# Paired state products, 64x64 prefix sums of bf16 parts, a decay row through DRAM and a new hand-written order in a gated recurrence followed by a bilinear FFN

## The chip, the cores and the metric

One core of a Trainium2 chip runs the whole program. The metric is the device time of one execution in microseconds (us), smaller is better. The engines of the core are named as in the profile: PE (matrix multiply), PEld (its weight loads), DVE (vector), ACT (scalar/activation), POOL, and SP, which here only issues DMAs. PE writes into PSUM, which has 8 banks of 512 f32 columns on 128 partitions; the program numbers them 0 to 7.

## What is computed

A gated linear recurrence over time for 4 batches x 8 heads (768 steps, head size 48), and a bilinear feed-forward layer on its output:

```python
for t in range(S):
    state = alpha[:, :, t, :, None] * state + np.einsum('bhd,bhe->bhde', k[:, :, t], v[:, :, t])
    y[:, :, t] = np.einsum('bhd,bhde->bhe', q[:, :, t], state)
x = y.transpose(0, 2, 1, 3).reshape(B * S, H * D)      # 3072 x 384
return ((x @ w_a) * (x @ w_b)) @ w_out                 # d_ff 1536
```

## The kernel before

The 768 steps of each batch are worked on in six chunks, numbered 0 to 5. A chunk is one third of the time of two of the four batches (its two "rows" u = 0, 1): 256 steps, held as 128 partitions of 2 neighbouring steps (r = 0, 1). The 128 partitions are two halves g = 0, 1 of 64, and the state is carried from half to half and chunk to chunk. In each chunk:

- the logarithms of alpha are taken (`ln`, ACT), the two steps of a partition are added (`l2`, DVE), and prefix sums over the partitions of each half are taken on PE by a triangular matrix. Chunk 0 sums the logarithms themselves in f32 (`B`, `cum_both`); chunks 1 to 5 split the sums into a high part (`H`, `high`, rounded to f32r) and a low part (`L`, `low`), and multiply each by the 128x128 triangular matrix `utr` (`A2`, `cum2`, lines 625-628): two matmuls of 384 columns for each of the two rows;
- exponentials of the sums (`E`) scale k and q (`mk`, `mq` on DVE, after `lv` has set the two steps of a partition to one level, on DVE or POOL) into `QKp`. `QKp` is transposed either on PE (`C`, `Ce`) or, from chunk 2 on, by a DMA transpose on SP's queue (`T`);
- the decay of each half, a column of `bls`, comes from PE and ACT (`dk`, `de`) in chunks 0 and 1, and from chunk 2 on by two small writes to DRAM and two reads (`dr`, `dl`, all on SP's queue);
- products of k and v that update the state: `K` for one half at a time (`state_pe`), `K2` with the matmuls of the two halves alternating (`state_pe_both`); then `k` on DVE;
- scores `D`, masked either on DVE (`M`) or by a copy on ACT and a product on DVE (`Mc`, `Mm`); the output of the chunk in PSUM (`SB`, `SA`, `Y`), and its copy to `xT` (`X`);
- the feed-forward layer of the chunk: `a f` and `b f` (3 matmuls each for one of 12 column blocks of `w_a` or `w_b`; 512 columns for a whole chunk, written `*`, 256 for one row), a copy of a to SBUF (`as`, ACT), the product (`pr`, DVE), and `o m 0`, `o m 1` (6 matmuls of 384 columns each), copied out (`ot`) and stored (`st`).

PE forms: the feed-forward matmuls, `B`, `A2` and `C` use all of the 128x128 array; `K`, `K2`, `D`, `SB`, `SA`, `Y` use 64x64 tiles, of which several run side by side; `dk` uses 128x48.

Nothing is scheduled by a compiler: `PROGRAM` (lines 17-405) is a list of these operations in one hand-written order, "chunk: operation arguments". Each engine and each DMA queue takes its own operations from that list in that order, and waits for what an operation needs. The last letter says who does it (V = DVE, S = ACT, P = POOL, Y = SP); for PE operations the last number is the PSUM bank. So where an operation stands sets its place in its engine's queue, and a late input holds up everything behind it on that engine. SP's queue has all stores, the DMA transposes, the DRAM trips of the decays and some loads; POOL's queue has the other loads, the loads of the weights (`W`, `Wo`) and some `lv`.

Example, chunk 2's preparation before the change (lines 104-119, lines of other chunks left out):

```
2: L * V
...
2: A2 1 1
...
2: E 1 i
...
2: A2 0 7
...
2: E 0 i
```

The functions `cross` and `cum_quads` (lines 606-623) are in the kernel before, but its order has no call of them.

Of the kernel before, what the change touches and what calls it, by code (L numbers as in the profile page):

```python
# [233 lines left out]
2: b 10 * 5; as 9 *; a 10 * 6; b 7 * 3; pr 9 *; as 10 *; o 0 0 0; pr 7 *; pr 10 *
3: D 1 1 6; D 1 0 1
4: lv 1 k P
3: M 1 1
2: o 0 1 -
3: Mc 1 0
5: ld q * P  # L240
3: Mm 1 0 V; SB 0 3
2: ot 0 S
3: SB 1 1; D 0 1 5
4: lv 1 q V; A2 0 0
2: o 2 0 7
# [12 lines left out]
3: X 0 S; X 1 V
2: o 2 1 -
4: mq 0 V; A2 1 2  # L260
2: ot 2 S
3: a 2 * 5
5: l2 * V
3: b 4 * 3
4: E 1 b; E 0 i; E 1 i
3: b 3 * 4; a 4 * 7; b 2 * 2
4: v 1 S
3: as 2 *
4: dr
5: H * S  # L270
2: ot 3 S
5: ra 0
2: st 0 Y
4: mk 0 V
3: as 4 *
4: mk 1 V
2: st 2 Y
3: a 8 * 1
4: T 0
3: a 1 * 0; a 0 * 6; b 8 * 7; as 8 *; b 5 * 5; pr 2 *; pr 4 *  # L280
4: v 0 V; dl
5: lv 0 q V
3: pr 8 *
4: mq 1 V
5: lv 0 k V
3: as 0 *
5: ra 1
3: a 3 * 1; a 5 * 3; b 0 * 7; a 9 * 6; as 5 *; pr 5 *; a 7 * 3; a 11 * 5; pr 0 *; as 9 *; as 3 *; as 1 *
4: T 1
3: b 9 * 6; b 1 * 1  # L290
5: lv 1 q V
3: pr 9 *; a 6 * 2; pr 3 *; as 11 *; pr 1 *; as 6 *
4: K * 0 0; D 0 0 4
5: L * V
3: as 7 *; b 11 * 6; b 6 * 7; pr 11 *; a 10 * 1; pr 6 *
4: Mc 0 0
2: o 1 0 5
3: as 10 *
4: k * 0 V; D 1 0 3; D 1 1 6; D 0 1 1
5: v 1 S  # L300
4: Mc 1 0; M 1 1
5: A2 0 0
2: o 1 1 -
4: SB 0 6; Mc 0 1; Mm 0 0 V; SB 1 3
2: ot 1 V
5: A2 1 2
3: b 7 * 1
5: E 1 i; E 1 b; E 0 b
3: b 10 * 5
4: Mm 0 1 V; Mm 1 0 V  # L310
3: pr 7 *; o 1 0 2
5: mk 1 V
3: pr 10 *; o 2 0 1
5: mq 1 V
4: Y 1; SA 0
5: dr
2: st 3 Y
5: T 1
4: Y 0; SA 1; X 1 S
5: E 0 i  # L320
3: o 1 1 -; o 2 1 -
4: X 0 V
5: mk 0 V; mq 0 V
3: ot 1 S
4: a 6 * 0; a 7 * 5; as 6 *
5: T 0
4: b 6 * 3; as 7 *; a 1 * 6
5: dl
4: pr 6 *; a 0 * 5; b 7 * 7; pr 7 *
3: ot 2 V; st 1 Y  # L330
4: as 0 *; as 1 *; a 5 * 3; b 1 * 4; b 0 * 2
2: st 1 Y
3: st 2 Y
4: pr 1 *; as 5 *; pr 0 *
5: v 0 V
4: a 3 * 0; a 4 * 7; as 3 *
5: D 0 0 5
4: as 4 *
5: K * 0 4; M 0 0; D 1 1 2; D 1 0 0; Mc 1 1
3: o 3 0 7  # L340
5: k * 0 V; Mc 1 0
3: o 3 1 -
5: SB 1 5
3: ot 3 S
5: SB 0 3; D 0 1 0
4: b 10 * 2
3: o 0 0 7
5: M 0 1; Mm 1 0 V; Mm 1 1 V
4: b 3 * 1; b 4 * 0
3: o 0 1 -  # L350
4: pr 4 *; b 5 * 0
3: ot 0 S
5: SA 1
4: pr 5 *
5: Y 1; Y 0
4: pr 3 *
5: X 1 V; SA 0
4: a 2 * 7; a 10 * 6
5: X 0 S
4: as 10 *; as 2 *; a 8 * 5  # L360
5: a 4 * 3
4: b 2 * 0
3: st 0 Y
5: a 2 * 4
4: pr 2 *; as 8 *; a 9 * 7
5: b 2 * 1; a 11 * 0
4: pr 10 *; b 8 * 5
5: as 2 *; as 4 *; a 1 * 4
4: b 9 * 2; pr 8 *
5: pr 2 *; b 5 * 3; b 1 * 6  # L370
4: as 9 *
5: b 4 * 1; a 8 * 5
4: a 11 * 7
5: pr 4 *
4: pr 9 *
# [10 lines left out]
5: a 9 * 4  # L386
4: o 3 0 7
5: b 9 * 2; pr 3 *
4: ot 0 V; st 0 Y
3: st 3 Y  # L390
4: ot 1 S
5: as 9 *
# [645 lines left out]
```

## Time and profile before

| | us |
|---|---|
| median of 3 runs (lowest, highest) | 195.91 (194.92, 201.03) |
| the profiled execution's own time | 195.05 |
| its span, first to last instruction | 193.3 |
| PE busy | 187.9 |
| DVE busy | 132.9 |
| ACT busy | 106.3 |
| POOL busy | 51.4 |

The span is the time between the first and the last instruction; about 1.75 us of the execution's own time lie around it. Busy times of engines overlap and don't add up to the span. The granted clock of PE is 1.000 over the span. In what follows "row" without more means a row of the profile, and "row 0/1 of a chunk" its two batches.

### The profile page before, as it was taken

How to read it: one execution, taken by the hardware profiler on the slowest of the kernel's cores; microseconds unless marked ns; L12 is line 12 of the kernel's file. 1: busy time of each engine (PE TensorE's matmuls, PEld its weight loads, DVE VectorE, ACT ScalarE, POOL GpSimd, SP SyncE). 2: the span in 40 equal slices, each digit the busy share in tenths (PEclk: the TensorE clock that was granted, in tenths of full speed). 3: DMA queues.
4: the chain of work that ended last, by engine and by line, in shares of the span. 5: the costliest groups of instructions: out<-in, count | busy, mean ns of one | idle time of the engine just before them, and what ended most of it. 6: DMA issues, size and time to landing. Idle time of an engine off the chain costs nothing.

```text
span 193.3 us, 5977 instructions
## 1 busy us (share of the span) xinstructions
PE 187.9 (97%) x2582; PEld 117.7 (61%) x2582; DVE 132.9 (69%) x221; ACT 106.3 (55%) x197; POOL 51.4 (27%) x69
## 2 busy tenths in 40 slices
PE   7989999999999999999999999999999999999993
PEld 3878875566888876644557544656455644455562
DVE  2498787988898879579787877896585525543311
ACT  4638785656859786645547775853462353431311
POOL 8999649260927003600007400000000000000000
PEclk9999999999999999999999999999999999999999
DMA  5999999999976989999598999006950100000342
GB/s 144 268 215 226 244 244 226 261 249 266 243 211 116 187 210 303 120 272 191 110 288 194 143 227 113 0 4 79 183 127 0 44 3 0 0 0 0 131 148 93
DMA packets 57034, 29.40 MB, mean 152 GB/s; under 512 B 47560, under 2 KB 54600, under 8 KB 57008
## 3 DMA queue, kind: packets, MB, share of 16 engines
q0 software_dynamic: 19056, 15.73, 44.2%
q1 hardware_dynamic: 37808, 13.19, 31.2%
q8 instruction: 20, 0.33, 0.7%
q10 hardware_dynamic: 144, 0.10, 0.2%
q14 instruction: 6, 0.05, 0.1%
HBM read 25.98 MB, written 4.74 MB: 159 GB/s over the span
## 4 chain that ended last, share of the span: by engine, by line
PE 91%; DMA 3%; POOL 2%; ACT 1%; DVE 1%; issue 1%; POOLq 0%; DVEq 0%
PE psum L864 48%; PE psum L886 24%; PE psum L810 7%; DMA a_t<-in_alpha_dram 3%; PE psum L786 3%; PE psum L628 2%; PE psum L707 2%; PE psum L744 2%; PE psum L897 1%; PE psum L687 1%; PE psum L588 1%; PE psum L589 1%; PE psum L757 1%; POOL v_t L547 0%; ACT la L554 0%
## 5 line engine op out<-in xcount | busy, mean ns | idle before, releaser
L864 PE MATMUL psum<-xT,wb_t 128*128 128x512 bf16 (+1 forms) x270 | 56.0, 337 | 0.0
L864 PE MATMUL psum<-xT,wa_t 128*128 128x512 bf16 (+1 forms) x270 | 55.5, 337 | 0.0
L886 PE MATMUL psum<-wo_t,prod 128*128 128x384 bf16 x276 | 49.5, 326 | 0.0
L864 PEld LDWEIGHTS <-wa_t 128*128 128x128 bf16 x270 | 25.9, 98 | 19.7 <-issue 0.2
L864 PEld LDWEIGHTS <-wb_t 128*128 128x128 bf16 x270 | 25.7, 98 | 20.0 <-issue 0.6
L886 PEld LDWEIGHTS <-prod 128*128 128x128 bf16 x276 | 26.0, 98 | 18.3 <-issue 0.5
L901 ACT ACTIVATE ot<-psum 128x384 f32<-128x384 f32 (+1 forms) x20 | 9.5, 480 | 19.5 <-PE psum L886 15.8
L642 POOL TENSOR_TENSOR k_t<-k_t,a_t 128x384 f32<-128x384 f32 x8 | 9.6, 1200 | 37.3 <-DMA k_t<-in_k_dram 35.9
L795 ACT ACTIVATE m<-psum 128x1024 bf16<-128x1024 f32 x15 | 15.1, 1022 | 4.6 <-PE psum L786 4.3
L791 DVE TENSOR_TENSOR m<-psum,mask 128x1024 bf16<-128x1024 f32 x9 | 10.9, 1216 | 3.2 <-PE psum L786 3.2
L554 ACT ACTIVATE la<-a_t 128x1536 f32<-128x1536 f32 (+2 forms) x9 | 9.5, 1055 | 5.6 <-DMA a_t<-in_alpha_dram 5.5
L845 ACT ACTIVATE xT<-psum 128x768 bf16<-128x768 f32 x8 | 6.5, 810 | 8.8 <-PE psum L810 8.7
L666 DVE TENSOR_TENSOR QKp<-k_t,invb 128x768 bf16<-128x768 f32 x10 | 9.4, 951 | 2.4 <-issue 1.5
L799 DVE TENSOR_TENSOR m<-m,mask 128x1024 bf16<-128x1024 bf16 x15 | 10.7, 736 | 0.1
L810 PE MATMUL psum<-m,vx 64*64 64x128 bf16 x576 | 10.2, 217 | 0.2 <-DVE m L799 0.2
L666 DVE TENSOR_TENSOR QKp<-q_t,beta 128x768 bf16<-128x768 f32 x10 | 10.0, 998 | 0.1
L786 PE MATMUL psum<-kqT 64*64 64x128 bf16 x384 | 9.7, 219 | 0.3 <-DVE kqT L715 0.2
L810 PEld LDWEIGHTS <-vx 64*64 64x64 bf16 x576 | 8.9, 107 | 1.0 <-issue 0.8
L547 POOL DMA_DIRECT2D v_t<-in_v_dram x8 | 8.4, 1051 | 0.1
L786 PEld LDWEIGHTS <-kqT 64*64 64x64 bf16 x384 | 6.7, 106 | 2.3 <-issue 1.9
L810 PE MATMUL psum<-kqT,Sm 64*64 64x128 bf16 x144 | 7.6, 220 | 0.1
L642 POOL TENSOR_TENSOR q_t<-q_t,ra 128x384 f32<-128x384 f32 x4 | 4.1, 1026 | 13.4 <-ACT m L795 13.1
(264 smaller groups left out, 281.1 us busy)
## 6 DMA issues: line engine op xcount, KB each, us to landing
out_dram<-ot SPq DMA_DIRECT2D x23, 192.0 KB, 2.9
a_t<-in_alpha_dram POOLq DMA_DIRECT2D x3, 768.0 KB, 13.8
q_t<-in_q_dram POOLq DMA_DIRECT2D x3, 768.0 KB, 8.7
k_t<-in_k_dram POOLq DMA_DIRECT2D x2, 768.0 KB, 11.7
v_t<-in_v_dram POOLq DMA_DIRECT2D x4, 384.0 KB, 6.2
k_t<-in_k_dram SPq DMA_DIRECT2D x2, 768.0 KB, 6.3
a_t<-in_alpha_dram POOLq DMA_DIRECT2D x3, 384.0 KB, 9.1
q_t<-in_q_dram POOLq DMA_DIRECT2D x3, 384.0 KB, 13.6
```

Of the source, the lines that this page charges most:

```text
L547: eng.dma_start(out=t[:, us, hs].rearrange("p b h r d -> p (b h) (r d)"), in_=src[ch.b0 + us.start:ch.b0 + us.stop, hs, ch.s * 2 * C:(ch.s ...
L554: nc.scalar.activation(out=ch.la[:, us, hs].rearrange("p b h r d -> p (b h r d)"), in_=ch.a[:, us, hs].rearrange("p b h r d -> p (b h r d) ...
L642: eng.tensor_mul(x, x, by)
L666: eng.tensor_mul(QKp[ch.c % 2][:, u, j, :, hs, :D], src[:, u, hs].rearrange("p h r d -> p r h d"), f)
L786: nc.tensor.matmul(s2[g * HC:(g + 1) * HC, r, p, rk, :], lhsT=ch.kqT[u][rs, 1, rk, 2 * h + p, g * HC:(g + 1) * HC], rhs=queriesT(ch, u, 2 ...
L791: nc.vector.tensor_mul(m.rearrange("p r a k s -> p (r a) (k s)"), ch.s2[u, h].rearrange("p r a k s -> p (r a) (k s)"), maskn(4))
L795: nc.scalar.activation(out=m.rearrange("p r a k s -> p (r a) (k s)"), in_=ch.s2[u, h].rearrange("p r a k s -> p (r a) (k s)"), func=AF.Copy)
L799: eng.tensor_mul(x, x, maskn(4))
L810: nc.tensor.matmul(y[c * DP:(c + 1) * DP, g, j // 2 * C:(j // 2 + 1) * C], lhsT=lhsT, rhs=rhs, start=(g, c) not in begun, stop=False, skip ...
L864: nc.tensor.matmul(p, lhsT=(wa_t, wb_t)[w][:, kk, f * 128:(f + 1) * 128], rhs=ch.xT[:, kk, us, :], start=(kk == 0), stop=(kk == KT - 1))
L886: nc.tensor.matmul(op, lhsT=ch.prod[:, f, at:at + C], rhs=wo_t[:, f, :], start=(f == 0), stop=(f == NFF - 1))
L901: nc.scalar.activation(out=o_, in_=i_, func=AF.Copy)
```

## The change

What it does, part by part:

- `K2` takes the two rows apart (`K2 0 0`, `K2 1 1`, `K2 * *`), and is used for both rows of chunks 1, 2 and 3. Before, it was used for row 0 of chunk 1 and for chunk 3; row 1 of chunk 1 and chunk 2 used `K`.
- In chunks 2 to 5, `H`, `L` and `A2` are replaced: `sw` (`cross`) copies row 1's sums by two DMAs on SP's queue with the two halves exchanged; `R 0`, `R 1` (`rest`, DVE) subtract the upper 16 bits of each f32, read as bf16; and `AQ` (`cum_quads`) multiplies three bf16 parts (the upper halves of the sums, of the rest and of the rest of that) by 64x64 blocks of a bf16 triangular matrix `utb`, 12 matmuls of 384 columns on the four 64x64 tiles of the array. The moving operand is every second bf16 of an f32 tile.
- In chunk 1, the decay of row 1 goes through DRAM (`dr 1`, `dl 1`); `dk` and `de` do row 0 alone. `bls` has another order of its axes.
- A new order of the whole program, with other banks and some operations on other engines. Counted over the program: `M` 9 to 8 and `Mc`/`Mm` 15 to 16; `ot` on DVE 5 to 9 and on ACT 18 to 14; `H` of chunk 1's row 0 from ACT to DVE; `cz` of `bls` and of the second `vxs` from POOL to DVE; chunk 3's k and chunk 4's q are loaded on SP's queue instead of POOL's.
- New functions for other forms (`decay_quads`, `turn_quads` and their like) are added and not called by the new order.

The core of the diff:

```diff
+    utb = cst.tile([C, C], BF16, name="utb")
...
-    bls = [cst.tile([C, B, P2], F32, name=f"bl{i}") for i in range(2)]
+    bls = [cst.tile([C, 2, 2, P2], F32, name=f"bl{i}") for i in range(2)]
...
     def cross(ch, eng):
-        ch.crossed = True
         for g in range(2):
             eng.dma_start(out=ch.l2[(1 - g) * HC:(2 - g) * HC, 2].rearrange("p h d -> p (h d)"),
                           in_=ch.l2[g * HC:(g + 1) * HC, 1].rearrange("p h d -> p (h d)"))
...
+    def top(t):
+        return t.bitcast(BF16).rearrange("p b h (d t) -> p b (h d) t", t=2)[:, :, :, 1]
+
+    def rest(ch, n):
+        name = ("lh", "ll")[n]
+        t = wk.tile([C, 2, H, D], F32R, name=name, bufs=1)
+        setattr(ch, name, t)
+        x, hi = (ch.l2[:, 0::2], top(ch.l2)[:, 0::2]) if n == 0 else (ch.lh.bitcast(F32), top(ch.lh))
+        nc.vector.tensor_sub(t.bitcast(F32).rearrange("p b h d -> p b (h d)"), x.rearrange("p b h d -> p b (h d)"), hi)
 
     def cum_quads(ch, i):
         p = wide(i)[:, :, :H * D]
         for u in range(2):
             ch.pf[u, 0, H] = p[:, u]
-        for t in (ch.lh, ch.ll):
+        for n, x in enumerate((top(ch.l2)[:, 0::2], top(ch.lh), top(ch.ll))):
             for u in range(2):
                 for g in range(2):
                     gs, to = slice(g * HC, (g + 1) * HC), slice((g ^ u) * HC, ((g ^ u) + 1) * HC)
-                    nc.tensor.matmul(p[to, u], lhsT=utr[gs, gs], rhs=t[gs, u].rearrange("p h d -> p (h d)"), start=(t is ch.lh), stop=(t is ch.ll))
+                    nc.tensor.matmul(p[to, u], lhsT=utb[gs, gs], rhs=x[gs, u], start=(n == 0), stop=(n == 2))
...
-    def decay_rows(ch):
-        ch.row = row = dram.tile([2, 2 * P2, 2, D], F32, name="row")
+    def decay_rows(ch, us):
+        if not hasattr(ch, "row"):
+            ch.row = dram.tile([2, 2, P2, 2, D], F32, name="row")
...
-    def state_pe_both(ch, us, t0, t1):
+    def state_pe_both(ch, us0, us1, t0, t1):
         i = ch.c % 2
-        for u in range(us.start, us.stop):
-            for g, tag in enumerate((t0, t1)):
+        pair = []
+        for g, us_, tag in ((0, us0, t0), (1, us1, t1)):
+            for u in range(us_.start, us_.stop):
                 ch.kv[u, g] = bank(tag)
...
+            pair.append([(u, p, rk, r) for u in range(us_.start, us_.stop) for p in range(P2) for rk in range(2) for r in range(2)])
+        for both in zip(*pair):
+            for g, (u, p, rk, r) in enumerate(both):
+                gs = slice(g * HC, (g + 1) * HC)
+                e = (u * P2 + p) * D
+                nc.tensor.matmul(ch.kv[u, g][r * DP:(r + 1) * DP, e:e + D], lhsT=QKp[i][gs, u, 1, rk, 2 * p + r, :], rhs=vxs[i][gs, u, rk, 2 * p + r, :D], start=(rk == 0), stop=(rk == 1))
```

Stretches of the new order that the prediction speaks of (the weights and chunk 1; chunk 2's preparation; the end):

```diff
+0: Wo 0 6
+1: ld k 1 P
+0: b 8 * 1
+1: lv 0 q P; ld q 1 P
+0: c3 P; cs 0 0 P; as 8 *; cs 1 0 V; Wo 6 12; pr 1 1; b 9 * 4; cz 1 q V
...
+1: C 0 1 0; dr 1; C 0 0 6; Ce 0 0 S
...
+1: v 1 V; K2 1 1 5 6
+0: o 2 0 4
+2: l2 * V
+1: M 1 0; X 0 S; a 4 0 3; a 3 0 7; as 3 0; a 5 0 2; b 3 0 1; dl 1; as 5 0; k 1 0 V
...
+2: sw Y
+0: st 3 Y
+1: as 1 0; as 4 0
+2: R 0; ld v * P
+1: b 1 0 5; pr 1 0; a 10 0 6
+2: ld q * P; lv 0 k P
+1: a 2 0 4; b 4 0 3; b 2 0 2; a 11 0 7; Mc 1 1; as 10 0
+2: R 1
+1: as 2 0; b 10 0 5
+2: AQ 0
+1: pr 4 0; as 11 0; SB 1 3
...
+2: lv 0 q V
...
+2: mq 1 V
...
+2: T 1; dl
+1: as 2 1; as 11 1; as 5 1
+2: mq 0 V
...
+2: K2 * * 4 6
+1: as 7 1
+2: D 1 0 0
+1: as 10 1; pr 1 1
+2: D 1 1 2; k * 0 V; T 0
...
+2: D 0 0 2
...
+5: pr 1 *; b 11 * 1; o 0 0 3; oc 1 0 0 4; o 2 0 5; pr 11 *; pr 8 *
+4: ot 0 V; ot 3 S; st 2 Y
+5: o 3 0 1; oc 1 0 1 -; o 0 1 -; o 3 1 -; otc 1 0 V; o 2 1 -
+4: st 1 Y; st 0 Y; st 3 Y
+5: ot 0 S; oc 1 1 0 6; oc 1 1 1 -; st 0 Y; ot 3 S; ot 2 V; st 3 Y; stc 1 0 Y; otc 1 1 S; st 2 Y; stc 1 1 S
```

More of the change, by code (lines that the diff above doesn't have):

```diff
@@ new lines @@
+1: H 0 V
+0: pr 4 0; pr 3 1; as 5 1
+1: ln 1; l2 1 V
+0: as 0 1; a 2 1 6; b 5 1 4; b 4 1 7; b 0 1 2; a 1 1 1
+1: ra 0
+0: pr 5 1; as 4 1; pr 4 1; a 9 * 0; a 8 * 4
+1: H 1 V
+0: as 1 1; pr 0 1
+1: L 0 V
+0: b 1 1 7
+1: A2 0 2
+0: Wo 0 6
[3 more added lines that the diff above has]
+0: c3 P; cs 0 0 P; as 8 *; cs 1 0 V; Wo 6 12; pr 1 1; b 9 * 4; cz 1 q V
+1: L 1 V
+0: as 2 1; as 9 *
+1: E 0 i
+0: pr 8 *; a 7 * 0; pr 9 *
+1: A2 1 1
+2: ld a * P
+0: b 2 1 5
+1: E 0 b; ra 1; mq 0 V; lv 0 k V
+0: pr 2 1; as 11 *
@@ new lines @@
+1: mk 0 V; ld v 1 P; lv 1 k P; E 1 i
+0: as 7 *; b 7 * 7; a 10 * 3; b 11 * 2; a 6 * 5; as 6 *; b 10 * 4; cz 1 v V; pr 7 *
+1: E 1 b
+0: pr 11 *
+1: C 0 1 0; dr 1; C 0 0 6; Ce 0 0 S
+0: as 10 *
+1: v 0 S; Ce 0 1 V
+0: cz 1 b V; b 6 * 1; o 1 0 5
+1: dk 0 7
+0: pr 6 *; pr 10 *
+1: lv 1 q V; D 0 0 0; D 0 1 2; de 0; K2 0 0 4 6
+0: o 3 0 7
+1: k 0 0 V; Mc 0 1; mk 1 V; Mc 0 0; Mm 0 1 V; mq 1 V; SB 0 2
+0: o 0 0 4; o 3 1 -
+1: C 1 0 0; k 0 1 V
+0: ot 3 S
+1: Ce 1 0 S; C 1 1 6
+0: o 1 1 -; o 0 1 -
+1: Mm 0 0 V; D 1 0 0; Ce 1 1 V; Y 0; SA 0
@@ new lines @@
+1: as 10 1; pr 1 1
+2: D 1 1 2; k * 0 V; T 0
+3: sw Y
+0: st 0 Y
+3: ld q * Y
+2: k * 1 V
+1: o 2 0 5; a 6 1 4
+2: Mc 1 0
+3: ra 0
+1: o 2 1 -
+2: Mc 1 1
+1: as 6 1
+3: ra 1
+1: b 7 1 0; b 6 1 1; ot 2 S; pr 10 1
+2: Mm 1 1 V
+1: pr 7 1; pr 6 1; o 3 0 7
+3: R 0
+2: D 0 0 2
+3: R 1; ld k * Y
+2: Mc 0 0
+1: o 0 0 6
+2: SB 0 0; SB 1 4; D 0 1 2; M 0 1; Mm 1 0 V; Mm 0 0 V
+3: lv 1 q V
+1: o 3 1 -
+0: st 1 Y
+1: o 0 1 -
+4: ln *
+3: AQ 2
+1: ot 3 V
+2: SA 1; Y 1; Y 0; SA 0
+3: E 1 b; E 0 b
+1: o 1 0 7
@@ new lines @@
+2: X 0 V
+4: l2 * V
+3: E 0 i; lv 0 q V; lv 0 k P
+1: o 1 1 -
+2: X 1 S; b 5 * 5; a 5 * 1; b 0 * 0; a 0 * 2
+3: E 1 i
+0: st 2 Y
+1: ot 0 S
+4: ld q * Y
+2: as 0 *; as 5 *
+3: mq 0 V; mk 0 V
+2: a 3 * 3
+3: dr; ld v * P
+2: as 3 *
+3: lv 1 k P
+2: b 3 * 4
+4: ra 1; ra 0
+2: pr 0 *; b 10 * 2; a 10 * 6; as 10 *; a 9 * 0
+1: ot 1 V
+2: a 8 * 7; a 7 * 6; pr 3 *; pr 5 *
+4: sw Y
+2: as 9 *
+4: R 0; lv 1 q P
+2: a 2 * 5; b 6 * 1; b 9 * 0; a 6 * 3; as 7 *
+3: T 0; mq 1 V
+2: pr 10 *
+1: st 3 Y
+3: dl
@@ new lines @@
+2: b 7 * 6; b 2 * 4; pr 9 *
+3: mk 1 V
+2: as 2 *; as 6 *
+1: st 2 Y
+3: T 1
+2: pr 6 *; pr 7 *
+5: ld a * Y
+2: b 1 * 0; b 8 * 3; a 1 * 1; pr 2 *; as 1 *; a 4 * 5; b 4 * 6
+3: v 0 V
+4: R 1
+2: pr 1 *
+3: v 1 V
+2: as 8 *; as 4 *; a 11 * 2; b 11 * 5
+3: D 0 0 0
+2: pr 4 *; pr 8 *; as 11 *
+4: ld k * Y
+3: Mc 0 0
+4: lv 0 q P
+3: K2 * * 6 4
+2: pr 11 *
+3: k * 0 V
+5: ld k * Y
+1: st 0 Y
+3: D 1 0 2
+2: o 0 0 7
+3: Mc 1 0; k * 1 V; D 1 1 0; SB 0 5
+2: o 0 1 -
+3: SB 1 2; Mc 1 1
+5: ln *
+3: Mm 1 0 V; D 0 1 0
@@ new lines @@
+2: o 3 0 4
+3: M 0 1; Mm 0 0 V; Mm 1 1 V
+2: o 3 1 -; ot 0 S
+4: AQ 0
+2: ot 3 V
+3: SA 1; SA 0; Y 1
+5: ld v * P; l2 * V
+3: X 1 V
+4: E 0 b; lv 0 k V
+3: Y 0
+2: o 2 0 7
+4: E 1 i
+3: X 0 S
+4: E 1 b; E 0 i
+2: o 2 1 -
+4: mq 1 V
+5: v 0 S; ra 1
+3: a 8 * 3
+4: mq 0 V
+3: a 9 * 5; a 3 * 6; b 0 * 2
+4: ld v * P; lv 1 k P
+3: b 8 * 0; a 2 * 1; as 8 *; as 3 *
+2: ot 2 S
+5: ra 0
+4: mk 0 V
+5: sw Y
+3: a 11 * 4; b 3 * 3
+5: v 1 V
+3: pr 8 *
+4: mk 1 V
+3: as 9 *; a 4 * 5; b 9 * 7; b 11 * 0; pr 3 *; a 0 * 6; as 11 *; a 5 * 4; as 0 *
@@ new lines @@
+4: v 0 S
+3: pr 9 *
+5: R 0
+3: b 2 * 7; pr 11 *; as 2 *; a 1 * 3; b 5 * 0
+5: ld q * P
+3: a 6 * 1; b 4 * 6
+5: lv 0 k P
+3: as 4 *
+4: dr
+3: a 10 * 5; pr 0 *; pr 2 *
+5: lv 0 q V
+3: as 5 *; b 6 * 4; pr 5 *
+4: v 1 V
+3: b 1 * 0
+4: T 0
+3: pr 4 *; as 6 *
+4: D 0 1 1; D 0 0 6
+5: R 1
+3: pr 6 *; as 1 *
+2: st 3 Y
+4: T 1; Mc 0 1
+3: a 7 * 3; pr 1 *
+5: lv 1 k P
+2: o 1 0 4
+3: b 7 * 0; as 10 *; as 7 *
+4: D 1 1 2; M 0 0; Mm 0 1 V
+3: pr 7 *
+4: K * 0 1; Mc 1 1; dl; k * 0 V; D 1 0 5; Mc 1 0; Mm 1 0 V
@@ L326 @@
+1: st 1 Y
+2: o 1 1 -
+5: AQ 0
+2: ot 1 S; st 0 Y
+4: SB 0 2; SB 1 6
+5: E 0 i
+3: b 10 * 5
+4: Mm 1 1 V
+5: E 1 b; E 0 b; E 1 i
+3: pr 10 *; o 1 0 4
+5: lv 1 q P
+3: o 2 0 5
+5: mk 1 V
+4: Y 0; Y 1; SA 0
+5: mq 1 V
+4: X 0 S; SA 1
+5: mq 0 V; dr
+3: o 1 1 -; o 2 1 -
+4: X 1 S
+5: T 1
+4: a 7 * 1
+5: mk 0 V
+3: ot 2 V
+4: a 1 * 6; a 0 * 5; b 1 * 7; a 3 * 2; b 7 * 0; as 7 *; as 1 *; pr 1 *
+3: ot 1 V
+4: b 0 * 3; a 6 * 7
+2: st 2 Y
+4: pr 7 *
 5: T 0
-4: b 6 * 3; as 7 *; a 1 * 6
+4: as 0 *
+2: st 1 Y
@@ L379 @@
[L379 to L404 removed]
+4: pr 0 *
@@ new lines @@
+5: D 1 1 0
+4: a 4 * 4
+5: M 1 0
+4: as 4 *; as 3 *
+3: o 0 0 3
+5: D 0 1 4; K * 0 6
+4: as 6 *
+5: Mc 0 1; M 1 1; D 0 0 1
+3: o 0 1 -
+5: k * 0 V
+4: b 6 * 0
+3: ot 0 S
+4: b 4 * 7
+5: SB 1 5; SB 0 3; Mc 0 0
+3: o 3 0 2
+4: pr 4 *
+5: Mm 0 1 V
+4: b 3 * 1; pr 3 *
+3: o 3 1 -
+4: a 5 * 1
+5: Y 1; Mm 0 0 V
+4: pr 6 *
+3: st 2 Y
+5: SA 0; Y 0; SA 1; X 0 V
+4: as 5 *; b 5 * 0
+3: ot 3 S
+4: b 11 * 7
+5: X 1 V
+4: a 10 * 2
+5: b 4 * 5; a 4 * 6
+4: b 10 * 1; as 10 *
+5: as 4 *
+4: pr 10 *; a 9 * 2; pr 5 *; a 8 * 6; as 8 *; a 2 * 3; as 9 *
@@ L559, in pairs @@
         us, hs = us
+        ch.apart -= set(range(us.start, us.stop))
         x = ch.la[:, us, hs].rearrange("p b h r d -> p (b h) r d")
@@ L593, in high @@
             ch.lh = wk.tile([C, 2, H, D], F32R, name="lh", bufs=1)
-        o_, i_ = (t.rearrange("p b h d -> p b (h d)") for t in (ch.lh[:, us], sums(ch, us)))
+        o_, i_ = (t[:, us].rearrange("p b h d -> p (b h d)") for t in (ch.lh, ch.l2))
         if eng is nc.scalar:
@@ L964 @@
         "A2": lambda x, u, i: cum2(x, int(u), i),
+        "R": lambda x, n: rest(x, int(n)),
         "AQ": lambda x, i: cum_quads(x, i),
```

524 lines of the change are left out of this document (139 added, 385 removed).

## The prediction

> **What bounds the kernel now.** I read the page first (busy shares, then the chain that ended last), then the waits of PE, then the chain in order of time, then busy times by stretch and the landings of DMAs.
>
> ```profile
> span 193.3 us, 5977 instructions
> ...
> PE 187.9 (97%) x2582; PEld 117.7 (61%) x2582; DVE 132.9 (69%) x221; ACT 106.3 (55%) x197; POOL 51.4 (27%) x69
> ...
> PE 91%; DMA 3%; POOL 2%; ACT 1%; DVE 1%; issue 1%; POOLq 0%; DVEq 0%
> ```
>
> PE is 97% busy and 91% of the chain. Busy alone proves little, so the list of PE's waits (who, for whom: us in total, times, longest):
>
> ```profile
> PE psum L571 <- DVE og L475: 1.2, 1, 1.2
> PE psum L588 <- ACT la L554: 0.2, 1, 0.2
> PE psum L810 <- DVE m L799: 0.2, 1, 0.2
> PE psum L786 <- DVE kqT L715: 0.2, 1, 0.2
> ```
>
> After its start PE waits 0.6 us in all. So the change gains what matmul time it takes out, and pays in full for each new wait of PE. The chain in order of time (start, length, what) has the prices of PE's work:
>
> ```profile
> 37.11 0.82 PE psum L687 x32
> ...
> 70.50 0.98 PE psum L886 x6
> 71.48 0.33 PE psum L864 x3
> 71.80 0.35 PE psum L786 x16
> 72.15 0.50 PE psum L744 x32
> 72.65 1.08 PE psum L886 x6
> ...
> 74.19 0.22 PE psum L786 x16
> ...
> 76.47 0.35 PE psum L628 x2
> 78.62 0.55 PE psum L628 x2
> ...
> 94.41 0.63 PE psum L757 x64
> ```
>
> L687 is a decay, L744 and L757 the state products without and with alternation, L628 one prefix sum of one row, L786 scores on 64x64 tiles. The last view is the busy time of the engines from 48 to 72 us, where chunk 2 is prepared (columns: stretch, length, PE, PEld, DVE, ACT, POOL, clock, DMA share, GB/s):
>
> ```profile
> 48.00:72.00 24.00, 24.00 (x412) 19.95 (x404) 20.45 (x39) 18.60 (x42) 9.46 (x8) 1.00 1.01 192
> ```
>
> PE is full, DVE has 3.55 us of 24 free, and the DMA engines are full too.
>
> **PE's own work, part by part.**
>
> Change of tile form. Sixteen score matmuls take 0.35 us behind full-array work (71.80) and 0.22 behind 64x64 work (74.19); six `o` matmuls take 1.08 behind 64x64 work (72.65), 0.98 otherwise (70.50). So each change between the full array and tiles costs 0.10 to 0.13 us; I take 0.10. Counted in the two orders, PE changes form 52 times before and 60 after: +0.80 us.
>
> Prefix sums of chunks 2 to 5. Removed are 8 pairs at L628. Rows show 0.35 to 0.55; the long ones stand next to tiles and hold a change of form, already counted, so 8 x 0.35 = 2.80 us. One matmul of 384 columns is then 0.175. Added are 4 x 12 matmuls of 384 columns on four tiles. Scores, also on four tiles, take 0.22/16 = 14 ns for 128 columns, so 41 ns for 384, and 12 x 41 = 0.49; a quarter of 0.175 each gives 0.53. I take 0.51, in all 2.04. Gain 0.76. The bounds: two tiles at a time, 12/2 x 0.175 = 1.05 each (a loss of 1.40); one at a time, 2.10 each (a loss of 5.6). No row has a moving operand that takes every second bf16. The nearest is L628, whose operand steps by the same 4 bytes and runs at 0.175, so I take full speed.
>
> The Trainium skill has a rule that speaks against this part. Its page "TensorEngine Tiling (Array Packing)", section "Restrictions and Gotchas", says that different row tiles cannot access one PSUM bank at the same time, and the new matmuls put both row tiles of a row u into bank u. In the order before, the four tiles that run together put the two row halves into two banks, so no run here shows it. By the rule the four prefix sums would come to 4.20 us, and the sum below to 2.16 more.
>
> State products. 0.50/32 = 15.6 ns without alternation (72.15), 0.63/64 = 9.8 with it (94.41). It is new for 64 matmuls of chunk 2 and 32 of chunk 1's row 1: 96 x 5.8 ns = 0.56 us gained. Bounds 0.4 to 0.6: in chunk 1 some already ran between scores.
>
> Decay of chunk 1's row 1. `dk` of both rows is 0.82 for 32 instructions (37.11); half goes: 0.41 gained. In its place come two writes and two reads on SP. The nearest rows are the chunk 2 reads of the row (median 2.8 us to landing). `dr 1` stands 13 us of PE's work ahead of `k 1 0`, which needs the result, so that is hidden by PE and costs nothing; if SP were held up, `k 1 0` on DVE would wait, and the products behind it.
>
> Sum: 2.80 - 2.04 + 0.56 + 0.41 - 0.80 = 0.93 us gained.
>
> **The other engines and queues.** To place steps I added PE's prices along each order up to each operation; I call that its place. In the trace an operation at place 36 to 63 runs 5.2 us later than its place (`o 3 1`: place 35.9, start 41.1).
>
> DVE. Each `R` is a subtraction like L604 (0.97 us; 128x768); eight are added (7.7 us), against four `L` (3.9) and two `H` on DVE (0.56 each, chunks 3 and 4). ACT loses two `H` (0.85). Four more `ot` (0.56) move to DVE, and one `M` (1.22) becomes `Mm` (0.74) with a copy on ACT. Over the whole, DVE gains some 4 us on 133 and ACT loses, and PE hides that. But between places 43 and 67 the orders have 35 and 42 DVE instructions, 20.9 and 26.6 us by their rows. Neighbours overlap by about 0.07 us (a 0.56 us product starts 0.48 after the one before), so 26.6 - 42 x 0.07 = 23.7 us of 24. The cover that the row above shows is used up.
>
> `sw` for chunk 2. Two DMAs of 96 KB on SP. They can start when `l2` is done, by DVE's rows at about 48 us. The nearest rows are stores of 192 KB, 2.9 us to landing, and 192 KB loads at 4.8, so they land at 51 to 53. `R 0` gets its turn on DVE at about 52; `AQ`, at place 49.6 (54.8 us), follows `R 1` by 0.6. Cost 0, bound +1.5; behind a waiting `R 0` stand the products `pr` that free PE's banks. In chunks 3 to 5 four places or more lie between what `sw` needs and `R 0`.
>
> Transposes of chunk 2. `mq 1` moves from place 52.5 to 55.5, `mq 0` from 55.7 to 57.5, the scores hardly (63.0 to 62.4). Before, `T 1` was issued at 58.6 and landed at 63.1, 5 us ahead of its scores (68.3). After, with 2 us queued on DVE, `mq 1` ends near 62.7 and `T 1` lands (4.5 to 5.5) at 67.2 to 68.2, scores due at 67.6. `T 0` is issued after it and after the reads of the decay, at 66.3 to 67.9, and lands at 70.8 to 73.5; due at 72.2. So PE waits 0 to 1.3 us; I take 0.3.
>
> Loads. POOL's loads land in order; the two halves of w_out land at 35.0 and 38.5, then chunk 1's k and q of row 1, 1.5 us each. The second half is now queued behind those: 41.5, used first at place 37.6 (42.7). `W b 768` lands about 1 us later (29.8), used at place 25.5 (30.3). No cost, bound 1 us in all. SP takes two loads from POOL (chunks 3 and 4), each over 10 us ahead of its use.
>
> Head and tail. PE is held up to 9.0 us by k's first half, last of SP's six loads in both orders, and to 11.8 by alpha's second row, POOL's second load in both; one `fill` less changes nothing there. ACT's weight of masks moves, hidden by those two. At the end the last whole-row block is computed 1.0 us before PE's end instead of 2.0, so its store starts later; the last store is the same half row on ACT's queue. Cost 0, bound +0.6.
>
> So 195.05 (profiled execution: span 193.3 and 1.75 around it) - 0.93 + 0.3 = 194.4. The median of the runs shown is 0.4% above that execution; the forecast is for executions like it.
>
> **Rivals.**
>
> - Two tiles at a time in the new sums: matmuls of the two row halves that write one bank take turns, or the strided operand runs at half speed. For it: no row shows two row halves in one bank. Against: four tiles run side by side everywhere else. 194.4 + 4 x (1.05 - 0.51) = 196.6. Chance 0.12. (The first of the two is what the Trainium skill's page "TensorEngine Tiling (Array Packing)", section "Restrictions and Gotchas", would have.)
> - One tile at a time: 194.4 + 4 x (2.10 - 0.51) = 200.8. Nothing in the rows looks like it. 0.03.
> - On the other side, slower: DVE as the bound of chunk 2's preparation. Its 23.7 of 24 us leave no room; late `mq` makes late transposes, and PE stands before the scores of chunk 2, then before `Y`, whose masks are DVE's next work (due within 0.6 us). It decides once DVE is over 1 us later than I reckon, for then the gain is gone. A lateness of 3 us gives 197, of 5 us 199. For it: the count above. Against: from 84 to 96 us DVE was 10.49 of 12 busy before, and PE waited for nothing. 0.22, of which 0.10 beyond 199.
> - Better than the sum: some of the small gaps at 18 to 24 us (12 `b` matmuls took 1.67 instead of 1.31) vanish, and `T` lands in time: 193. 0.10. Below 191.1 only if nearly all 3 us of such gaps from 4 us on went: 0.03 more.
>
> **How the numbers follow.** The forecast, 193.5 to 195.5, has 0.50; two tiles 0.12; DVE 0.22; one tile 0.03; better 0.13. The range from 192.5 to 198.5 leaves out the one-tile case, the far end of the DVE case and the far end of the better one: together under 0.2. About 2% either way (under 191.1, over 199.0) is what a measurement of this kernel can tell from no change: faster 0.03, slower 0.13, the rest 0.84.
>
> **What would show it.** Right: the prefix sums take about 0.5 us each on PE; 64 state products of chunk 2 take about 0.63; the decay of chunk 1 is 0.41; PE busy falls by 1 us; waits of PE stay under 1 us. Wrong: prefix sums of 1 us or more; a wait of PE for `kqT` or for `m` in chunk 2; DVE waiting at `R 0` for the DMAs; a gap of PE before its first `o 3 1`. The sum fails if a new wait of over 1 us stands in the list of PE's waits.

## The result and the profile after

| | before | after |
|---|---|---|
| median of 4 runs each, same chip (us) | 195.64 | 198.16 |
| lowest, highest (us) | 194.92, 201.03 | 196.98, 198.75 |
| the profiled execution's own time (us) | 195.05 | 198.75 |
| its span (us) | 193.3 | 196.9 |

The 201.03 us is a slow execution of the kernel before, and the ratio leaves it out. The ratio of the runs is 1.014, 95% interval 1.0099 to 1.0181: slower by 2.7 us, where 0.65 us faster was forecast. So 3.4 us have to be found. The page of after, the lines that answer to those of before:

```profile
span 196.9 us, 6049 instructions
...
PE 188.5 (96%) x2597; PEld 116.2 (59%) x2597; DVE 140.0 (71%) x233; ACT 102.7 (52%) x190; POOL 48.3 (25%) x64
...
PE 73%; DMA 13%; DVE 8%; issue 3%; POOL 1%; SPq 1%; ACT 0%; POOLq 0%; DVEq 0%
```

PE is still 96% busy, but its part of the chain has fallen from 91% to 73%, and DMA has risen from 3% to 13%: the end now hangs on transfers. The waits of PE and then of DVE in after (who, for whom: us in total, times, longest; lines left out between):

```profile
PE psum L905 <- DVE prod L919: 3.1, 3, 2.3
PE psum L561 <- DVE og L459: 1.2, 1, 1.2
PE psum L827 <- DVE kqT L730: 0.5, 2, 0.4
PE psum L785 <- DVE vx L773: 0.3, 1, 0.3
```

```profile
DVE lh L609 <- DMA l<-l: 2.8, 1, 2.8
DVE k_t L638 <- DMA k_t<-in_k_dram: 2.1, 1, 2.1
DVE Sm L812 <- DMA bl<-row: 1.6, 1, 1.6
...
DVE Sm L816 <- DMA bl<-row: 0.7, 1, 0.7
```

The second list explains the first. L609 is `R 0` of chunk 2. It stands on DVE until the exchange (`l<-l`) has landed, and the products `pr` (L919), which free PE's banks, are queued behind it. So PE's wait is put down to `prod`, though `prod` is a short instruction: the DMA is one step further back. The chain of after in order of time (start, length, what) names it:

```profile
40.10 0.46 PE psum L686 x16
...
49.12 0.17 SPq L598
...
49.33 6.97 DMA l<-l
...
71.45 0.64 PE psum L798 x64
...
80.73 0.63 PE psum L619 x12
```

Seven us pass from the issue of the second exchange DMA until `R 0` goes on; the first packet of the exchange ran only at 52.1. The other three lines are the gains: half a decay in 0.46 (0.82 before for a whole one), 64 state products in 0.64, and a prefix sum of both rows in 0.63, change of form included (0.54 to the next operation's start). Laid against the undisturbed durations of its matmuls, PE loses 2.5 us at 53 to 58 us, 0.9 us at 59 to 70, 1.05 us at 111 to 126 (behind chunk 4's `k_t`, issued at 99.87 on SP and landed at 111.7), and some 0.5 us more than before at the head. This execution is the slowest of its four, 3.7 us above that of before, so its losses come to more than the 3.4 us of the runs.

### The profile page after: what moved, and what is told of

Read it like the earlier page. It is cut to its first block, busy times and chain, and to the rows that moved or that the text cites. A ratio compares the mean times of both kernels' runs of the same rounds, so it can differ in the third digit from the quotient of the medians.

```text
span 196.9 us, 6049 instructions
## 1 busy us (share of the span) xinstructions
PE 188.5 (96%) x2597; PEld 116.2 (59%) x2597; DVE 140.0 (71%) x233; ACT 102.7 (52%) x190; POOL 48.3 (25%) x64
## 4 chain that ended last, share of the span: by engine, by line
PE 73%; DMA 13%; DVE 8%; issue 3%; POOL 1%; SPq 1%; ACT 0%; POOLq 0%; DVEq 0%
PE psum L905 38%; PE psum L927 19%; DMA k_t<-in_k_dram 6%; PE psum L851 5%; DMA l<-l 4%; DMA v_t<-in_v_dram 3%; DVE QKp L664 3%; PE psum L827 3%; DVE prod L919 3%; PE psum L722 1%; PE psum L938 1%; PE psum L785 1%; DVE ll L609 1%; PE psum L578 1%; PE psum L579 1%
## 5 line engine op out<-in xcount | busy, mean ns | idle before, releaser
L905 PE MATMUL psum<-xT,wb_t 128*128 128x512 bf16 (+1 forms) x270 | 56.3, 337 | 2.8 <-DVE prod L919 2.7
L927 PE MATMUL psum<-wo_t,prod 128*128 128x384 bf16 x276 | 50.1, 327 | 0.0
L836 ACT ACTIVATE m<-psum 128x1024 bf16<-128x1024 f32 x16 | 16.1, 1024 | 5.7 <-PE psum L827 5.7
L638 POOL TENSOR_TENSOR k_t<-k_t,a_t 128x384 f32<-128x384 f32 x7 | 8.4, 1205 | 39.5 <-DMA k_t<-in_k_dram 39.4
L942 ACT ACTIVATE ot<-psum 128x384 f32<-128x384 f32 (+1 forms) x15 | 7.2, 481 | 13.0 <-PE psum L927 10.8
L664 DVE TENSOR_TENSOR QKp<-k_t,invb 128x768 bf16<-128x768 f32 x10 | 11.0, 1111 | 0.0
L638 POOL TENSOR_TENSOR q_t<-q_t,ra 128x384 f32<-128x384 f32 x5 | 5.6, 1132 | 21.5 <-ACT ra L631 10.4
L832 DVE TENSOR_TENSOR m<-psum,mask 128x1024 bf16<-128x1024 f32 x8 | 9.7, 1218 | 1.6 <-PE psum L827 1.6
L944 DVE COPY ot<-psum 128x384 f32<-128x384 f32 (+1 forms) x10 | 5.3, 530 | 6.6 <-PE psum L927 4.5
```

Of the source, the lines that this page charges most:

```text
L638: eng.tensor_mul(x, x, by)
L664: eng.tensor_mul(QKp[ch.c % 2][:, u, j, :, hs, :D], src[:, u, hs].rearrange("p h r d -> p r h d"), f)
L832: nc.vector.tensor_mul(m.rearrange("p r a k s -> p (r a) (k s)"), ch.s2[u, h].rearrange("p r a k s -> p (r a) (k s)"), maskn(4))
L836: nc.scalar.activation(out=m.rearrange("p r a k s -> p (r a) (k s)"), in_=ch.s2[u, h].rearrange("p r a k s -> p (r a) (k s)"), func=AF.Copy)
L905: nc.tensor.matmul(p, lhsT=(wa_t, wb_t)[w][:, kk, f * 128:(f + 1) * 128], rhs=ch.xT[:, kk, us, :], start=(kk == 0), stop=(kk == KT - 1))
L927: nc.tensor.matmul(op, lhsT=ch.prod[:, f, at:at + C], rhs=wo_t[:, f, :], start=(f == 0), stop=(f == NFF - 1))
```

## The experiments

The theories, with the letters that an expectation may use: (A) the late exchange of chunk 2 is the loss, and (A1) it is late because POOL's loads keep the DMA engines full; (B) DVE has too much work in chunk 2's preparation; (C) the trip of chunk 1's decay through DRAM holds SP up; (D) the head and chunk 4's late k make up a good part. Each run is set against runs of the kernel before on its own chip (medians there 195.43, 195.58 and 195.66 us in three groups); the ratio is what compares.

| run | edit | median us | ratio to before, 95% |
|---|---|---|---|
| after | | 198.16 | 1.014 (1.0099 to 1.0181) |
| e1 | no exchange in chunk 2 | 194.91 | 0.9972 (0.9949 to 0.9995) |
| e2 | chunk 2's v and q loaded later | 197.03 | 1.0089 (1.0058 to 1.012) |
| e3 | chunk 1's decay all on PE | 197.89 | 1.0137 (1.0103 to 1.0171) |
| e4 | head, and chunk 5's alpha earlier | 198.34 | 1.015 (1.0122 to 1.0178) |
| f1 | e1, products not alternating | 195.96 | 1.003 (1.0003 to 1.0056) |
| f2 | no exchange in chunks 2 to 5 | 196.79 | 1.0061 (1.0041 to 1.0081) |
| f3 | chunk 2's exchange on ACT's queue | 204.71 | 1.0466 (1.0423 to 1.0509) |
| f4 | chunk 2's exchange earlier | 201.41 | 1.0311 (1.0269 to 1.0353) |
| g1 | e1, chunk 4's k on POOL | 202.48 | 1.0324 (1.0278 to 1.037) |
| g2 | chunk 4's k on POOL | 204.39 | 1.0434 (1.0382 to 1.0486) |
| g3 | e1 again | 195.18 | 0.9978 (0.9956 to 1.0) |
| g4 | exchange on ACT's queue in time | 198.24 | 1.0119 (1.0077 to 1.0162) |

### e1: chunk 2 without the exchange

```diff
-2: sw Y
...
+        at = slice(0, 2) if ch.c == 2 else slice(0, 3, 2)
...
+                    to = gs if ch.c == 2 else to
```

Row 1 of chunk 2 is summed as it lies, so only two tiles run side by side. `R 0` and `R 1` stay.

> The changed kernel, but chunk 2's sums are taken without the exchange of halves by two DMAs (each row's matmuls stay on their own half, two tiles at a time); DVE's subtractions stay. Theory A (PE stands near 56 us because the exchange's DMAs land 7 us after their issue and DVE waits 2.8 us for them before R 0): DVE's wait is gone, PE's wait of 2.3 us with it, chunk 2's prefix sum takes 1.0 us instead of 0.6, and the time falls by 1.5 to 2.2 us, from 198.2 to about 196.3. Theory B (DVE has too much work between 48 and 72 us): DVE's work is the same, so PE's wait stays above 1.5 us and the time within 0.5 us of 198.2.

Measured: 194.91 us, 1.7% below after and just below before. The waits of PE in e1, whole list, and a piece of its chain:

```profile
PE psum L560 <- DVE og L458: 1.2, 1, 1.2
PE psum L829 <- DVE kqT L732: 0.4, 1, 0.4
```

```profile
55.60 1.05 PE psum L621 x6
```

No wait for `prod` is left, nor the loss at 111 us. `R 0` starts at 52.66 on DVE, the turn that the prediction gave it ("about 52"), instead of 56.40. It gained more than expected, 3.3 us of the missing 3.4, although chunk 2's sum now takes 1.05 us. In the two traces the same matmuls start 2.5 us earlier in e1 at 72 us (70.01 instead of 72.55) and 3.5 us earlier at 122 (118.38 instead of 121.87): the late exchange costs about 2.5 us by then, net of e1's slower sum, and some 1.0 us more comes at 111 to 122 us. DVE does the same work as in after, the exchange apart, so (B) is out. Busy times from 48 to 72 us (stretch, length, PE, PEld, DVE, ACT, POOL, clock, DMA share, GB/s), after and then e1:

```profile
48.00:72.00 24.00, 21.39 (x393) 17.30 (x384) 18.72 (x36) 15.81 (x37) 4.47 (x4) 1.00 0.90 165
```

```profile
48.00:72.00 24.00, 23.88 (x415) 19.19 (x404) 20.86 (x41) 17.66 (x39) 4.36 (x4) 1.00 0.93 175
```

DVE has 3.1 us of 24 free in e1, while PE is full.

### e2: POOL's loads out of the way

```diff
-2: R 0; ld v * P
+2: R 0
...
-2: ld q * P; lv 0 k P
+2: lv 0 k P; ld v * P; ld q * P
```

> The changed kernel, but POOL issues chunk 2's loads of v and q only behind lv 0 k of chunk 2, that is some 10 us later, when chunk 2's k has landed. Theory A1 (the exchange lands late because POOL's loads keep all DMA engines full): it lands within 4 us of its issue instead of 7, DVE's wait before R 0 falls from 2.8 to under 0.7 us, PE's wait falls from 2.3 to under 0.7, and the time falls by 1.5 to 2.3 us to about 196.2. Theory A2 (it is late by itself, from its own 128 rows or from SP's queue): it still lands about 7 us after its issue and the time stays within 0.5 us of 198.2.

Measured: 197.03 us. The DMA issues from 44 to 60 us (KB each, median us from issue to landing), after and then e2:

```profile
l<-l SPq DMA_DIRECT2D x2, 96.0 KB, 6.4
```

```profile
l<-l SPq DMA_DIRECT2D x2, 96.0 KB, 2.8
```

The same two DMAs, issued at the same time (48.4 against 48.7), land in 2.8 us once POOL's queue has nothing for them to stand against. DVE no longer waits for `l<-l`, PE's loss at 53 to 58 us is gone, and the prefix sum starts at 55.4 instead of 58.2. That is (A1) for the lateness of the exchange; how much time the lateness costs is what e1 shows. The profiled execution gains 2.2 us of span, the median only 1.1: with v and q later, PE loses 1.04 us at 59 to 69 us and 0.4 at 72, and near 99 us it stands 0.5 us for a transpose of chunk 3. That this is the price of the later loads is likely, but was not taken apart.

### e3: no trip of the decay

```diff
-1: C 0 1 0; dr 1; C 0 0 6
+1: C 0 1 0; C 0 0 6
-1: dk 0 7
+1: dk * 7
```

(and `de *` for `de 0`, `dl 1` left out)

> The changed kernel, but the decay of both rows of chunk 1 comes from PE and ACT, as before; no write and read of row 1 through DRAM. If the trip through DRAM only takes its place (theory A): PE has 0.41 us more, DVE's wait of 1.6 us for the decay near 51 us is gone but is spent at R 0 instead, whose DMA lands when it did; time +0.2 to +0.5 us, about 198.6. If the 768 packets of 4 bytes and the wait of DVE are what makes the exchange late (theory C): the exchange lands 1 to 3 us earlier and the time falls by 1 us or more, to 197.2 or less.

Measured: 197.89 us, no different from after. With no decay read ahead of it on SP, the exchange still came late:

```profile
DVE lh L609 <- DMA l<-l: 3.9, 3, 2.7
```

So (C) is not the cause. The trip itself took 6.9 us for its reads instead of the 2.8 that I had put in, but with or without it the time is the same.

### e4: head and chunk 5's alpha

```diff
-0: fill 2 5; mk 0a V; de 0; v 0 V; C 0 0 4; W a 256 768; Ce 0 1 V; cs 1 m V; W a 0 256; Ce 0 0 V; K 0 0 5; D 0 1 0; k 0 0 V; W b 0 256; W b 256 768; D 0 0 6
+0: fill 2 5; mk 0a V; Ce 0 1 S; de 0; v 0 V; C 0 0 4; W a 256 768; cs 1 m V; W a 0 256; Ce 0 0 V; K 0 0 5; D 0 1 0; k 0 0 V; W b 0 256; W b 256 768; D 0 0 6
...
 4: sw Y
+5: ld a * Y
...
 3: T 1
...
-5: ld a * Y
```

> The changed kernel with two moves: the first copy of a transposed block of chunk 0 (Ce 0 1) is on ACT, as before, instead of DVE behind the cast of v; and chunk 5's load of alpha stands on SP's queue behind chunk 4's exchange instead of behind chunk 3's second transpose. Theory D: the first costs 0.5 us at the head (the first prefix sums of row 1 start at 11.8 instead of 12.4), the second delays chunk 4's load of k (lands at 111 us, 11.8 after its issue), DVE waits 2.1 us for it and PE loses 1.0 us; so the time falls by 1.2 to 1.6 us to about 196.8, and k lands before 107 us. Rival: the head is set by the landing of v and nothing is gained there, and the loss near 111 us is DVE's backlog and stays: within 0.4 us of 198.2.

Measured: 198.34 us, nothing gained, so (D) is not borne out. In its lists of waits (PE, then DVE):

```profile
PE psum L827 <- DMA kqT<-QKp: 1.1, 1, 1.1
```

```profile
DVE Sm L812 <- DMA bl<-row: 2.3, 1, 2.3
```

DVE no longer waits for chunk 4's k, but the alpha now runs ahead of the transposes of chunk 3, and PE stands 1.1 us for those near 101 us instead of losing 1.05 us at 111. The loss was moved, not removed. The first move did not help the head: the first prefix sums of row 1 start at 13.07 us, in after at 12.43. And as DVE stands 2.3 us for chunk 1's decay, it comes later to `R 0` and stands only 0.8 us for the exchange there. So this run does not tell what the head and the late k cost.

### f1: e1 without the new alternation

```diff
-1: v 1 V; K2 1 1 5 6
+1: v 1 V; K 1 0 5; K 1 1 6
-2: K2 * * 4 6
+2: K * 0 4; K * 1 6
```

> Chunk 2 without exchange as in e1, and the alternation of the state products undone in chunk 2 and in row 1 of chunk 1 (96 matmuls one half after the other). If the matmul terms of the forecast are time of the program and not only of PE: 96 x 5.8 ns = 0.56 us more than e1 (194.9), so 195.5. Rival: PE's gain is given back at the next wait, the time stays at 194.9. In the trace the 64 products of chunk 2 should take 1.0 us instead of 0.64.

Measured: ratio 1.003 against 0.9975 of the two runs of e1, 1.1 us with an uncertainty of some 0.6. The expected 0.56 lies in it, and the rival's 0 does not, which speaks for a gain of the program; how large it is the runs tell only roughly. The profiled execution is the slowest of f1's twelve and also has waits of PE that e1 has not (1.0 us for a transpose, 1.0 us for `la` at the head). The products of chunk 2 in the chain of f1, and then of e1:

```profile
68.93 0.93 PE psum L787 x57
```

```profile
68.84 0.64 PE psum L800 x64
```

That is 16.3 ns for one without alternation and 10 with it; 15.6 and 9.8 were forecast.

### f2: no exchange anywhere

The lines `3: sw Y`, `4: sw Y`, `5: sw Y` go as well, and `to = gs` holds for all.

> No exchange of halves in any of chunks 2 to 5; all four prefix sums run two tiles at a time. If the exchange pays where it has time (chunks 3 to 5): 3 x (1.05 - 0.54) = 1.5 us more than e1 (194.9), so 196.4. Rival: the exchanges of chunks 3 to 5 cost as much elsewhere (loads and transposes behind them on SP's queue, DVE's waits for k of chunk 4), and without them the time stays within 0.5 us of e1.

Measured: 196.79 us, ratio 1.0061, so 1.7 us above e1; 1.5 were expected. Where four places or more lie between `sw` and its use, the exchange pays all that the four tiles save.

### f3 and g4: the exchange on ACT's queue

f3:

```diff
-2: sw Y
+2: sw S
```

> As the changed kernel, with the exchange of chunk 2 issued on ACT's queue instead of SP's. If full DMA engines make it late (POOL's loads), it lands as late as on SP, 55 to 56 us, DVE waits 2 to 3 us for it, and the time stays at 198.2. Rival, SP's queue as the cause (the exchange stands behind the decay read that lands at 51): it lands at 52 to 53 and the time falls to 195.5.

Measured: 204.71 us, which neither theory had. ACT came to the issue only at 52.8 us, behind copies that wait for PE, so the queue was not what this run compared. It shows instead what a later exchange costs. The waits of PE and of DVE:

```profile
PE psum L905 <- DVE prod L919: 7.1, 2, 6.9
```

```profile
DVE lh L609 <- DMA l<-l: 8.7, 1, 8.7
```

5.9 us more for `R 0` make PE wait 4.0 us more, and 6.5 us more in all (for the rest see the granted clock in the last section). g4 puts the issue right behind the pair sums, so that ACT gets to it in time:

```diff
-2: l2 * V
+2: l2 * V; sw S
...
-2: sw Y
```

> The changed kernel with the exchange of chunk 2 on ACT's queue, right behind the pair sums, so that ACT issues it at 48.7 as SP did. If POOL's loads on the DMA engines make it late: 6.4 to 7.3 us from issue to landing, 55 to 56 us, and 198.2 us in all (ACT loses 1.1 us to the issue, which may add 0.5). Rival, SP's queue: 2.8 us from issue to landing, no wait of DVE for it, 195.5.

Measured: 198.24 us, as after. ACT issued it at 48.8 and 49.3, SP in after at 48.7 and 49.3; the first packet ran at 52.1 in both, and `R 0` started at 56.5 and 56.4. DVE's wait in g4 is that of after. PE waits less for `prod` (1.9 us instead of 3.1), but 0.9 us for a copy on ACT, which now issues the exchange:

```profile
DVE lh L608 <- DMA l<-l: 2.7, 1, 2.7
```

```profile
PE psum L904 <- DVE prod L918: 1.9, 2, 1.5
...
PE psum L904 <- ACT xT L885: 0.9, 1, 0.9
```

So it is not SP's queue that makes the exchange late, nor the decay reads that stand before it there.

### f4: issuing the exchange earlier

```diff
+2: ln *
 0: ot 3 S
...
+2: l2 * V; sw Y
 1: Ce 1 1 V; Y 0; SA 0
-2: ln *
...
-2: l2 * V
...
-2: sw Y
```

> As the changed kernel, with the logarithms of chunk 2, the pair sums and the exchange about 2.2 us earlier in ACT's, DVE's and SP's order, so that the exchange is issued at 46.5 instead of 48.7. If it takes 7 us from issue wherever it stands under POOL's loads: it lands at 53.5 to 54, DVE waits 0.5 to 1 us, the time is 196.2. If POOL's queue holds the engines until 52 whatever is queued: it lands at 55 to 56 again and the time stays at 198.2. Rival: the copy of chunk 1's transposes, 1 us later on DVE, makes PE stand before chunk 1's products, and the time is 197.

Measured: 201.41 us, a miss. The exchange was issued only 1.1 us earlier (47.6) and landed 6.4 and 7.0 us after its two issues (54.0 and 55.2 us), ahead of `R 0`, whose turn on DVE came only at 58.2. For on SP the exchange now stood ahead of `dl 1`, the read of chunk 1's decay, which I had overlooked. The waits of PE and of DVE:

```profile
PE psum L827 <- DVE prod L919: 4.3, 1, 4.3
```

```profile
DVE Sm L812 <- DMA bl<-row: 6.1, 1, 6.1
```

The same wait with another name: what comes on SP under POOL's loads lands 6 to 7 us after its issue, and whoever stands first in DVE's order pays.

### g1 and g2: chunk 4's k on POOL

```diff
-4: ld k * Y
+4: ld k * P
```

g1 is e1 with this edit, g2 the changed kernel with it.

> e1 (chunk 2 without exchange) with chunk 4's k loaded on POOL's queue again, as in the kernel before, some 9 us earlier than on SP's. e1 had a wait of 1.3 us on DVE for that k and lost nothing on PE by it: 194.7 to 194.9, DVE's wait gone. Rival: the load now lies under the DMA transposes of chunk 3, which land late as the exchange of chunk 2 did, PE waits 1 us or more for kqT near 98 us, and the time is 196.

> The changed kernel with chunk 4's k loaded on POOL's queue. If the 1.05 us that PE lost at 111 to 126 us in the changed kernel came from that load's lateness: 197.2, and DVE's wait of 2.1 us for it is gone. Rival: the same loss comes at another wait (kqT near 100 us), and the time stays at 198.2.

Measured: 202.48 and 204.39 us; both rivals held, at more than their price. The load moved from 99 to 88 us, onto the transposes of chunk 3. PE's waits in g1 and in g2:

```profile
PE psum L829 <- DMA kqT<-QKp: 2.5, 1, 2.5
```

```profile
PE psum L827 <- DMA kqT<-QKp: 4.3, 1, 4.3
```

DVE's wait for k is gone in both. It is the mechanism of chunk 2 in another place: with the load on POOL a DMA of SP is late. The second transpose of chunk 3 takes 7.6 us from its issue (93.75) in g1; in e1, issued at 93.33, it held nothing up when its scores began at 98.98. How much of the 1.05 us at 111 us in after was due to the late k stays open, since each edit that removed that wait made another; but e1 and e2, where DVE waits 1.3 and 1.8 us for that k, show no wait of PE there.

### g3: e1 again

> e1 once more, with more runs beside the kernel before: 0.997 of its time (195.0 us where that takes 195.6), the interval below 1.

Measured: ratio 0.9978; the first time it was 0.9972. The changed kernel without chunk 2's exchange is faster than the kernel before by about a quarter of a per cent. That is little: the interval, expected below 1, reaches 1.0 here and reached 0.9995 the first time.

## Why the prediction was wrong, step by step

- **`sw` of chunk 2: the step that failed.** It was put at "land at 51 to 53", "cost 0, bound +1.5". It landed at 55.1 and 56.3, DVE stood 2.8 us, PE 2.3, and taking it out gives 3.3 us (e1). The rows that priced it were a median over 23 stores of the whole program (2.9) and two loads at the start (4.8); in the trace of before SP issues no DMA between some 4 and 54.8 us, so no row stood in this place. A nearer one was there: two stores of 192 KB, issued at 81.8 and 82.2 us of before while POOL's loads ran. They took 6.1 us, though they also stood behind the decay's small writes on SP. The row of the stretch from 48 to 72 us that the prediction shows has the DMA share at 1.01, and the text says that the DMA engines are full; the price of the transfer did not use it. The sign that it names for being wrong, "DVE waiting at `R 0` for the DMAs", is what came.
- **Prefix sums: right.** 0.51 forecast, 0.54 measured, 1.05 with two tiles (e1), which was the bound. The rival with two tiles at a time is out. The rule of the Trainium skill's page "TensorEngine Tiling (Array Packing)", section "Restrictions and Gotchas", that different row tiles can't access one PSUM bank at the same time, would have made 1.05 of it; the trace of after, 0.63 for 12 matmuls with the change of form, does not bear it out for this use.
- **State products: right** (10 ns for 9.8; f1's time fits).
- **Decay of chunk 1: right on PE** (0.46 is left, 0.36 gained of 0.41). Its reads took 6.9 us, not 2.8, and DVE waited 1.6 us for them in after; that they are "hidden by PE" was wrong for DVE, but e3 shows no time in it.
- **The sum on PE.** e1 stands at 0.9975 of before, 194.6 by the profiled execution's 195.05. Its chunk 2 pays 0.51 for the slow sum, so with an exchange that costs nothing the change would be near 194.1; 194.4 was forecast. By the time of the runs the sum held, and one cost was missing. The busy time of PE does not confirm it: "PE busy falls by 1 us" did not come (187.9 before, 188.5 in after), and e1 and g3, which are one kernel, show 188.4 and 187.4, so this figure is too coarse for a gain of 0.9.
- **DVE full in chunk 2: wrong, too high.** "23.7 of 24 us" were worked out, e1 shows 20.86 busy in that stretch with PE full. The rival that rested on it, at 0.22, gave the right side and nearly the right time (197 to 199) by the wrong mechanism: PE waited neither for a late transpose of chunk 2 nor for `m`. That the measured 198.16 lies within 192.5 to 198.5 is therefore luck. Over the whole program DVE is busy 7.1 us more, not "some 4"; among the rest, the 29 products into `QKp` take 2.1 us more than in before.
- **Transposes of chunk 2:** 0.3 taken; no wait of PE for them in after or in e1.
- **Loads:** "each over 10 us ahead of its use" was wrong for chunk 4's k, which DVE waited for (2.1 us): on SP it stands behind a transpose and an alpha, and took 11.8 us.
- **Head and tail:** cost 0, bound 0.6; some 0.5 us is lost at the head, and e4 did not get it back.

## What to carry to other kernels

Price a DMA by a row that runs against the same other loads, not by its size alone: under full DMA engines the same transfer took 6 to 7 us here in place of 3, whether SP or ACT issued it. Before a DMA is put between two instructions of one engine, look at what else stands behind the one that will wait, and set the transfer's distance from its use by the crowded price. A transfer that stalls in one chunk can pay in the next: here three of four exchanges pay 0.5 us each, and the fourth cost 3.3.

## What the runs showed of the hardware

**A DMA of SP or ACT under POOL's loads starts late, and runs slowly.** The exchange of chunk 2 (two DMAs, each of 64 packets of 1536 bytes), by the DMA packets of the traces, in us. On SP a store of 192 KB follows with packets of the same size, which can't be told apart, so in SP's rows the last column holds the store too; on ACT the exchange stands alone:

| run | queue | issued | first packet | last packet ends (on SP with the store) |
|---|---|---|---|---|
| after | SP | 48.7, 49.3 | 52.1 | 56.0 |
| f4 | SP | 47.6, 48.2 | 51.4 | 55.3 |
| g4 | ACT | 48.8, 49.3 | 52.1 | 55.5 |
| f3 | ACT | 52.8, 53.4 | 56.6 | 60.7 |
| e2, v and q of POOL later | SP | 48.4, 49.0 | 49.6 | 52.2 |

Under POOL's loads 3.3 to 3.8 us pass before the first packet, 1.2 without; then the packets of the exchange alone take 3.4 and 4.1 us (ACT), and exchange and store together 3.9 us on SP under the loads, against 2.6 without. The Trainium skill's page "DMA: Bandwidth & Descriptors", section "Queues, rings and completion order", says that a DMA engine takes turns between its queues, packet by packet. That would slow the exchange, but it does not say why nothing of it runs for over 3 us; these traces don't show why either.

**A wait of PE can cost twice.** In g1 the `o` matmuls behind the wait of 2.5 us at 98 us run at half speed (six take 2.0 us; behind 64x64 work they take 1.08). Busy times of g1 (columns as in the stretches above: the clock is the third from the end):

```profile
98.00:102.00 4.00, 1.52 (x96) 1.12 (x89) 3.65 (x7) 1.04 (x2) 3.26 (x3) 0.84 1.29 200
102.00:108.00 6.00, 6.00 (x74) 3.08 (x71) 0.76 (x2) 3.91 (x4) 0.00 (x0) 0.54 1.45 201
```

The granted clock falls to 0.54 for the next 6 us and is 1.00 from 108 on. f3 has 0.50 and 0.58 from 60 to 70 us after its wait of 6.9; after kept 1.00 through its wait of 2.3. g2 has 0.75 from 102 to 108 us, with its wait of 4.3. So in g1, g2 and f3 the price is not the wait alone, and the times went past the prices expected. Nor is it set by the length of the wait alone: added up over such stretches, the clock that was not granted is about 3.4 us in g1, 1.7 in g2 and 5.1 in f3. The Trainium skill's page "TensorE: Matmul & The Clock Gate", part "The HAM clock gate", has the clock halve after an idle window of about 3.4 us; here a wait listed at 2.5 us was enough.
